# Spreading the normalisers of four heads from DRAM by two transfers, one for each query part, in place of four

## The chip, the cores and the metric

The kernel runs on one core of one Trainium2 chip. The metric is the device time of one execution in microseconds (us); lower is better. Each comparison runs the kernel before on the same chip beside the other kernel, so its median differs a little from job to job (294.9 to 301.2 us).

## The reference, cut to what matters

An attention with forget gates feeds a channel mix. Batch 8, 8 heads, 576 positions, 64 dimensions a head; the mix has 512 and 1024 channels. Only the division by the row sum matters here.

```python
scores = np.where(causal, -1e9, scale * q @ k.T + decay)
attn = np.exp(scores - scores.max(-1, keepdims=True))
attn = attn / (attn.sum(-1, keepdims=True) + 1e-09)   # the normaliser
x = (attn @ v)                  # heads side by side: (B, S, 512)
xk = mu_k * x + (1 - mu_k) * x_prev                   # and xr the same with mu_r
out = sigmoid(xr @ w_r) * (relu(xk @ w_k) ** 2 @ w_v)
```

## The kernel before

Heads go in pairs (32 pairs), and the normalisers in groups of two pairs, that is four heads. TensorE sums the weights into `den`; VectorE transposes the sums, takes reciprocals and transposes back, so that `R` holds one row of normalisers per head and query part. The product of weights and values has 64 rows (dimensions) for each of two heads, so one row of normalisers must be copied to 64 partitions. For the first two groups a matmul does that. For the other 14, `R` is stored to a DRAM tile `scr` and loaded back with each row repeated 64 times into `rb`. The queries are cut into part 0 (384 columns) and part 1 (192).

```python
PARTS = [(0, 384), (384, 192)]
QB = PARTS[0][1] // 32
mm_ring = Ring(3, [P, 512], F32, "mm", mmp)            # PSUM, three buffers
scr_ring = Ring(2, [4, 32, 32 * QB], F32, "scr", drp)  # DRAM
rb_ring = Ring(3, [P, 2, S], F32, "rb")
# ... cut ...
def spread_norm(g):
    scr = scr_ring()
    nc.sync.dma_start(out=scr.rearrange("g r c -> (g r) c"),
                      in_=R.rearrange("p a b -> p (a b)"))
    rb = rb_ring()
    for half, (q0, n) in enumerate(PARTS):
        for hh in range(2):
            nc.sync.dma_start(
                out=rb[hh * D:(hh + 1) * D, :, q0:q0 + n],
                in_=scr[2 * half + hh, 0:2, 0:n].unsqueeze(0).to_broadcast([D, 2, n]))
    for i in range(2):
        rbs[2 * g + i] = rb[:, i, :]
# ... cut ...
def values(Pi, half):
    nm = mm_ring()
    # ... cut: matmuls of weights and values into nm ...
    q0, n = PARTS[half]
    nc.vector.tensor_tensor(out=xs[Pi % NX][:, 1 + q0:1 + q0 + n], in0=nm[:, 0:n],
                            in1=rbs[Pi][:, q0:q0 + n], op=ALU.mult)
```

The multiply is L423 in the profile of the kernel before.

The softmax here doesn't subtract the row's maximum and nothing guards it: scores larger than these inputs give would overflow.

## Time and profile before

| | before |
|---|---|
| median time | 294.92 us (4 runs, 293.64 to 297.48) |
| profiled run | span 298.2 us, granted TensorE clock 0.977 |
| TensorE busy | 266.5 us, 89% |
| loads `rb<-scr` | 28 of 192 KB and 28 of 96 KB, 3.3 us to landing |
| wait of the multiply for them | 12.0 us in all |

The profiled run took 299.94 us, over 1.5% above the fastest run, so it counts as slow. In a row of the profile, `x<-mm,rb` means that the instruction writes tile `x` and reads `mm` and `rb`; the first pair of numbers is the busy time in us and the mean duration in ns, what follows the second bar is idle time of the engine just before, with what ended it. "SPq" is the queue that issues transfers.

### The profile page before, as it was taken

How to read it: one execution, taken by the hardware profiler on the slowest of the kernel's cores; microseconds unless marked ns; L12 is line 12 of the kernel's file. 1: busy time of each engine (PE TensorE's matmuls, PEld its weight loads, DVE VectorE, ACT ScalarE, POOL GpSimd, SP SyncE). 2: the span in 40 equal slices, each digit the busy share in tenths (PEclk: the TensorE clock that was granted, in tenths of full speed). 3: DMA queues.
4: the chain of work that ended last, by engine and by line, in shares of the span. 5: the costliest groups of instructions: out<-in, count | busy, mean ns of one | idle time of the engine just before them, and what ended most of it. 6: DMA issues, size and time to landing. Idle time of an engine off the chain costs nothing.

```text
span 298.2 us, 8098 instructions
## 1 busy us (share of the span) xinstructions
PE 266.5 (89%) x3194; PEld 159.0 (53%) x3221; DVE 226.1 (76%) x462; ACT 204.6 (69%) x360; POOL 88.0 (30%) x117
## 2 busy tenths in 40 slices
PE   1677878769899999999969999999989999999994
PEld 0344545335555655566535655566555656655551
DVE  6758989787978988789847977797968886874431
ACT  4878688457877878588865887688777875424530
POOL 7294227262333333223322424132322111000000
PEclk9999799978999999999988999999999999999999
DMA  7999996854759494939584594949471915131112
GB/s 211 237 258 202 242 230 190 206 142 146 208 150 262 126 300 121 282 112 270 151 240 135 150 274 119 278 114 290 115 223 65 250 35 185 65 115 70 68 41 106
DMA packets 82438, 52.06 MB, mean 175 GB/s; under 512 B 50336, under 2 KB 77216, under 8 KB 82400
## 3 DMA queue, kind: packets, MB, share of 16 engines
q1 hardware_dynamic: 80080, 48.75, 57.5%
q0 software_dynamic: 2096, 2.62, 5.1%
q8 instruction: 25, 0.41, 0.6%
q10 hardware_dynamic: 224, 0.18, 0.3%
q14 instruction: 13, 0.11, 0.1%
HBM read 41.96 MB, written 12.19 MB: 182 GB/s over the span
## 4 chain that ended last, share of the span: by engine, by line
PE 65%; DVE 11%; DMA 9%; ACT 9%; issue 2%; SPq 2%; DVEq 0%; ACTq 0%
PE mm L468 25%; PE mm L453 15%; PE mm L416 7%; PE sc L328 7%; DMA rb<-scr 6%; ACT a L334 5%; PE sc L233 4%; PE den L364 3%; PE mm L472 3%; ACT qkT L244 2%; DMA scr<-R 2%; SPq L386 2%; DVE x L423 2%; DVE a L340 2%; ACT rel L459 1%
## 5 line engine op out<-in xcount | busy, mean ns | idle before, releaser
L334 ACT ACTIVATE a<-sc 128x1024 bf16<-128x1024 f32 (+1 forms) x128 | 100.3, 842 | 17.0 <-PE sc L328 16.8
L453 PE MATMUL mm<-xk,wk_sb 128*128 128x288 bf16 x512 | 73.9, 289 | 1.5 <-DVE x L423 0.7
L468 PE MATMUL mm<-wv_sb,relusq 128*128 128x512 bf16 x246 | 61.4, 387 | 3.3 <-DVE x L423 2.7
L459 ACT ACTIVATE rel<-mm 128x288 bf16<-128x288 f32 x128 | 48.4, 417 | 16.4 <-PE mm L453 13.0
L453 PEld LDWEIGHTS <-wk_sb 128*128 128x128 bf16 x512 | 48.0, 99 | 21.0 <-issue 6.3
L220 POOL TENSOR_TENSOR vw<-vf,wbf 128x512 bf16<-128x512 f32 x32 | 34.5, 1077 | 72.8 <-DMA vf<-in_v_dram 30.1
L461 DVE TENSOR_TENSOR relusq<-rel 128x576 bf16<-128x576 bf16 x64 | 34.2, 544 | 28.0 <-ACT rel L459 27.9
L340 DVE TENSOR_TENSOR a<-a,bound 128x256 bf16<-128x256 bf16 (+2 forms) x96 | 44.7, 477 | 3.6 <-ACT a L334 3.3
L482 ACT ACTIVATE th<-mm 128x512 f32<-128x512 f32 x36 | 21.5, 598 | 34.7 <-PE mm L468 28.7
L328 PE MATMUL sc<-qkT 64*128 64x64 bf16 (+4 forms) x384 | 37.3, 291 | 8.2 <-ACT a L334 3.8
L468 PEld LDWEIGHTS <-relusq 128*128 128x128 bf16 x256 | 23.6, 99 | 32.2 <-issue 8.1
L244 ACT COPY qkT<-sc 128x1024 bf16<-128x1024 bf16 x29 | 29.4, 1014 | 14.8 <-PE sc L237 14.3
L423 DVE TENSOR_TENSOR x<-mm,rb 128x384 bf16<-128x384 f32 x64 | 27.1, 454 | 14.7 <-DMA rb<-scr 12.0
L209 POOL CAST qb<-qf 128x512 bf16<-128x512 f32 x22 | 18.1, 825 | 62.6 <-PE sc L233 37.4
L468 PE MATMUL mm<-wr_sb,xr 128*128 128x512 bf16 x111 | 32.6, 387 | 1.6 <-issue 0.3
L489 DVE SCALAR_TENSOR_TENSOR res<-th,mm 128x512 f32<-128x512 f32 x36 | 24.6, 683 | 12.4 <-PE mm L468 8.1
L328 PEld LDWEIGHTS <-qkT 64*128 64x128 bf16 x384 | 15.0, 96 | 30.3 <-issue 24.1
L416 PE MATMUL mm<-a,vw 128*32 128x192 bf16 (+3 forms) x896 | 29.5, 267 | 0.7 <-ACT rel L459 0.4
L441 DVE SCALAR_TENSOR_TENSOR xk<-diff,mu_k_sb,x 128x576 bf16<-128x576 bf16 x32 | 26.4, 826 | 1.1
L441 DVE SCALAR_TENSOR_TENSOR xr<-diff,mu_r_sb,x 128x576 bf16<-128x576 bf16 x32 | 26.0, 812 | 0.0
L416 PEld LDWEIGHTS <-vw 128*32 128x32 bf16 x896 | 20.4, 99 | 6.8 <-issue 4.4
L233 PE MATMUL sc<-ident,qb 128*128 128x128 bf16 x128 | 13.2, 230 | 8.4 <-DVE qb L209 5.3
(67 smaller groups left out, 237.0 us busy)
## 6 DMA issues: line engine op xcount, KB each, us to landing
out_dram<-res SPq DMA_DIRECT2D x36, 256.0 KB, 3.5
qf<-in_q_dram SPq DMA_DIRECT2D x32, 256.0 KB, 4.3
kf<-in_k_dram SPq DMA_DIRECT2D x32, 256.0 KB, 4.5
vf<-in_v_dram SPq DMA_DIRECT2D x64, 128.0 KB, 4.2
rb<-scr SPq DMA_DIRECT2D x28, 192.0 KB, 3.3
scr<-R SPq DMA_DIRECT2D x14, 192.0 KB, 1.9
rb<-scr SPq DMA_DIRECT2D x28, 96.0 KB, 3.3
vt_f<-in_v_dram SPq DMA_DIRECT2D x8, 128.0 KB, 5.4
```

Source lines behind the costliest of these rows:

```text
L220: nc.gpsimd.tensor_tensor(out=vw[Pi % NV], in0=vf[Pi % NV], in1=wbf[:, :4, 2 * Pi:2 * Pi + 2].unsqueeze(3).to_broadcast([P, 4, 2, D]), op= ...
L244: copy(qkT[Pi % NQK][:, lo * S:hi * S].rearrange("p (i s) -> p i s", i=n)[:, :, 0:4 * P] .rearrange("p i (j c) -> p i j c", c=4), tp[:, 4 ...
L328: nc.tensor.matmul(sc[:, hh, w:w + n], lhsT=t[lo:lo + D, S + kb * P:S + (kb + 1) * P], rhs=t[lo:lo + D, q0:q0 + n], start=True, stop=True)
L334: nc.scalar.activation(out=a[:, :, off:off + w], in_=sc[:, :, 0:w], func=AF.Exp, scale=SCALE)
L340: nc.vector.tensor_tensor(out=v_, in0=v_, in1=bound[:, o:o + w].unsqueeze(1).unsqueeze(1).to_broadcast([P, 2, n, w]), op=ALU.min)
L416: nc.tensor.matmul(nm[r0:r0 + 32, o:o + n], lhsT=w[:, d0:d0 + 32], rhs=a[:, hh, col:col + n], start=(kb == 0), stop=last, tile_position=(0 ...
L423: nc.vector.tensor_tensor(out=xs[Pi % NX][:, 1 + q0:1 + q0 + n], in0=nm[:, 0:n], in1=rbs[Pi][:, q0:q0 + n], op=ALU.mult)
L441: nc.vector.scalar_tensor_tensor(out=dst[:, p, :], in0=diff, scalar=mu[:, p:p + 1], in1=x[:, 0:S], op0=ALU.mult, op1=ALU.add)
L453: nc.tensor.matmul(kp[:, :HB], lhsT=wk_sb[:, db, fb * P:(fb + 1) * P], rhs=xks[b][:, db, hf * HB:(hf + 1) * HB], start=(db == 0), stop=(db ...
L459: nc.scalar.activation(rel[:, fb % 2, :], kp[:, :HB], func=AF.Relu)
L461: nc.vector.tensor_mul(rsq[b][:, fb - 1:fb + 1, hf * HB:(hf + 1) * HB], rel, rel)
L468: nc.tensor.matmul(ps, lhsT=tiles[b][:, i, t0:t0 + P], rhs=w[:, i, :], start=(i == 0), stop=(i == n - 1))
```

## The change

The intent is two issues in place of four for each group. A query part is fetched for both heads by one transfer onto all 128 partitions. For that, part 1 is padded to the width of part 0, so that the rows of both pairs of heads lie end to end (2 x 384 numbers, 3072 B) in DRAM and in `rb`.

```diff
-    rb_ring = Ring(3, [P, 2, S], F32, "rb")
+    rb_ring = Ring(3, [P, 2, 2, 32 * QB], F32, "rb")
 ...
-        for half, (q0, n) in enumerate(PARTS):
-            for hh in range(2):
-                nc.sync.dma_start(
-                    out=rb[hh * D:(hh + 1) * D, :, q0:q0 + n],
-                    in_=scr[2 * half + hh, 0:2, 0:n].unsqueeze(0).to_broadcast([D, 2, n]))
+        for half in range(2):
+            nc.sync.dma_start(
+                out=rb[:, half].rearrange("p j c -> p (j c)"),
+                in_=scr[2 * half:2 * half + 2, 0:2, :].rearrange("g j c -> g (j c)")
+                .unsqueeze(1).to_broadcast([2, D, 2 * 32 * QB]))
         for i in range(2):
-            rbs[2 * g + i] = rb[:, i, :]
+            rbs[2 * g + i] = rb[:, :, i, :]
 ...
-                                in1=rbs[Pi][:, q0:q0 + n], op=ALU.mult)
+                                in1=rbs[Pi][:, half, 0:n], op=ALU.mult)
```

The first four pairs and the views used at the start are adapted to the new shape in the same way (cut).

More of the change, by code (lines that the diff above doesn't have):

```diff
@@ L140 @@
     chain = [rb_ring() for _ in range(2)]
-    lf, cum, wrow, zrow = (chain[i // 2][:BH, i % 2, :] for i in range(4))
+    lf, cum, wrow, zrow = (
+        chain[i // 2].rearrange("p a b c -> p (a b c)")[:BH, i % 2 * S:i % 2 * S + S]
+        for i in range(4))
     nc.scalar.dma_start(out=lf, in_=f_bh[:, :])
@@ L397, in spread_now @@
             for i in range(2):
-                rbs[2 * g + i] = rb[:, i, :]
+                rbs[2 * g + i] = rb[:, :, i, :]
         for half, (q0, n) in enumerate(PARTS):
@@ L402, in spread_now @@
                              rhs=R.rearrange("p a b -> p (a b)")[:, 0:n], start=True, stop=True)
-            copy(rbs[Pi][:, q0:q0 + n], rp[:, 0:n])
+            copy(rbs[Pi][:, half, 0:n], rp[:, 0:n])
     def values(Pi, half):
```

## The prediction

In the text below k is the number of DMA engines that a transfer runs on. That the new form has k = 2 was supposition: nothing in the kernel before shows it. So are the reasons for the queueing and one of the three terms of the range, the one for the rate, because no trace shows them. 12.6 us of delay, less 1.5 for the work ahead, plus 1 for the queueing (a bare estimate) are 12.1 us a group; 14 groups make 169 us, and 295 + 169 = 464 was put at 460. The 28 us that it names as the new period are 15.9 + 12. The range of some -45 to +55 us came from all three terms, so it doesn't follow from the two that are left.

> **What bounds the kernel now.** I read the page of the kernel before first: engine shares, then the group of instructions that reads the tile `rb`, then the list of DMA issues.
>
> ```profile
> PE 266.5 (89%) x3194; PEld 159.0 (53%) x3221; DVE 226.1 (76%) x462; ACT 204.6 (69%) x360; POOL 88.0 (30%) x117
> ...
> L423 DVE TENSOR_TENSOR x<-mm,rb 128x384 bf16<-128x384 f32 x64 | 27.1, 454 | 14.7 <-DMA rb<-scr 12.0
> ...
> rb<-scr SPq DMA_DIRECT2D x28, 192.0 KB, 3.3
> scr<-R SPq DMA_DIRECT2D x14, 192.0 KB, 1.9
> rb<-scr SPq DMA_DIRECT2D x28, 96.0 KB, 3.3
> ```
>
> TensorE is the bound at 89%. The spread is 14 groups (four heads each) of one store `scr<-R` and four loads `rb<-scr`; one load lands 3.3 us after its issue. The multiply that eats the normalisers (L423, VectorE) already waits 12.0 us for these loads in all, so they have no slack. What such a wait does to TensorE I read from busy times by stretch, two undisturbed steady ones against one with the longest wait in it:
>
> ```profile
> core 0: us, PE busy (x) PEld busy (x) DVE busy (x) ACT busy (x) POOL busy (x), PEclk, DMA share, GB/s
> ...
> 149.31:165.90 16.59, 14.30 (x188) 7.92 (x186) 10.69 (x22) 10.62 (x20) 4.00 (x4) 0.90 0.62 176
> 182.00:215.00 33.00, 32.44 (x398) 19.28 (x401) 26.76 (x55) 25.40 (x46) 10.14 (x13) 1.00 0.70 197
> 215.00:248.00 33.00, 32.12 (x445) 19.26 (x449) 25.65 (x56) 26.02 (x48) 7.32 (x8) 1.00 0.51 145
> ```
>
> TensorE is 97 to 98% busy in the undisturbed stretches: there is no idle time in which a new delay could hide. The chain of work that ended last, at one group, shows the path:
>
> ```profile
> 144.90 0.58 DVE R L377
> ...
> 145.50 1.86 DMA scr<-R
> ...
> 147.38 0.58 SPq L386
> ...
> 149.31 5.35 DMA rb<-scr
> ...
> 154.74 0.38 DVE x L423
> ...
> 155.16 0.58 PE mm L468
> ```
>
> R is ready at 145.5, the store lands 1.86 us later, the first of four loads is issued at 147.38 and the fourth at 149.31, and it lands 5.35 us after that; the multiply frees a PSUM buffer of the ring of three and TensorE goes on. The timeline of VectorE and of the DMA queue gives the same for all groups. With t0 the start of the first load's issue, the multiply of query part 1 starts at t0 + 5.2 to 7.4 us, typically 5.7 (100.43 to 106.02, 115.43 to 121.25, 181.35 to 187.44), in 8 of 14 groups after a wait; the others have about 1 us to spare. From one t0 to the next it is (258.40 - 51.40) / 13 = 15.9 us.
>
> [...]here an issue takes 0.60 us (start-to-start 0.65) and the landing 3.3[...].
>
> **The change part by part.**
> 1. *Issues.* Two in place of four: the last one starts 2 x 0.65 = 1.3 us sooner.
> 2. *Bytes.* Query part 1 is padded from 192 to 384 columns. A group moves 2 x 384 = 768 KB in place of 2 x 192 + 2 x 96 = 576 KB; 14 groups make 2.75 MB more than now, 5% of the 52.06 MB. Rows are 3072 B in place of 1536 and 768 B: 256 in place of 512 per group.
> 3. *Engines.* This decides it. The old source pattern is [64 copies, 2, n], and the destination has 64 partitions: k = 16. The new source is [2, 64 copies, 768], and its slowest dimension is the 2 for the two heads; the destination's is 128. [...]both transfers use the same two engines, one after the other.
> 4. *Arithmetic and buffers.* The multiply, its shape, the copies of the first four pairs and the order of instructions stay. `rb` grows by 1.5 KB per partition and buffer: no time.
>
> The rate of one engine, as an estimate: I take the fastest slices of the DMA line. In 102 to 107 us (mostly loads) they are 367 to 385 GB/s, in the tail (stores only) up to 415.
>
> ```profile
> GB/s 233 295 258 246 221 270 258 320 270 197 197 135 184 141 49 86 154 123 117 98 137 111 96 156 170 178 221 279 309 352 385 352 334 324 365 367 340 324 315 291
> ...
> GB/s 306 0 0 5 11 22 5 0 38 410 251 22 0 0 0 0 0 0 0 0 0 377 322 0 0 0 0 27 377 295 0 0 0 0 38 415 246 0 0 0
> ```
>
> That is 24 to 26 GB/s per engine. A transfer of 393,216 B on two engines is 196,608 B each: 196,608 / 25,000 per us = 7.9 us. The fixed part: a 192 KB load lands in 3.0 us at the least, of which 196,608 / 385,000 = 0.5 us is data, so 2.5 us. First transfer: t0 + 2.5 + 7.9 = t0 + 10.4. Second, behind it: t0 + 18.3, against use at t0 + 5.7 now. **Delay: 12.6 us per group.**
>
> What of it reaches the end? Nearly all. VectorE works in order and stands still at L423, with masks, squares and results behind it; TensorE has the ring of three PSUM buffers, two of them held by the waiting products, so it does about one more unit. I take off 1.5 us for that work ahead. Then I add 1 us for queueing[...]. Sum: 12.6 - 1.5 + 1 = 12.1 us, times 14 groups = 169 us. 295 + 169 = 464 us; I say 460.
>
> **The rivals.**
> - *The transfers still use 16 engines* (the pattern reaches the hardware in a form with 64 or 128 outermost).[...] Then the second transfer is issued 1.3 us sooner, and of the 12.0 us of waits some 9 us go (each of the 8 waits at part 1 falls by at most 1.3, the first waits by some 0.6). Half reaches TensorE: 290 to 292 us, within 2%. I give this 13%.
> - *Padding costs.* 16 engines, but 33% more bytes in the spread land later in heavy load: 192 KB more at 375 GB/s is 0.5 us per group, at most 14 x 0.5 = 7 us, less the gain of the issues. Within 2% again.
> - *The two engines become the bound by themselves.* If all other traffic waits behind them and casts and value weights come late, the period is more than 28 us; 32 us would make 295 + 14 x 16 = 519. Against it: q, k and v are loaded two to four slots ahead of use, a slot being 8 us.
> - *The wait is hidden.* Against it: L423 already waits in most groups, and TensorE has no spare time.
>
> **Range and chances.** 460 us if k is 2. Within that case [...]the work ahead by 1.5, the queueing by -1 to +3; over 14 groups that is some -45 to +55. The range 405 to 515 leaves out the case of 16 engines, which I keep in the chances: faster 0.02, same 0.12, slower 0.86.
>
> **What would show it.** The list of issues should have `rb<-scr` x28 with 384 KB. Right: a median landing of 10 to 18 us; DMA slices of low busy share (2 of 16 engines, a tenth or two) and 50 GB/s while L423 waits; L423 waiting for `rb<-scr` some 150 to 190 us in all (12.0 now); PE busy time near 266 us, but its share falling to about 57%; t0 to t0 at 28 us. Wrong: a landing of 3 to 4 us means 16 engines, and the time stays near 291. A landing near 10 us for both would mean that they run side by side (the second on other engines), about 8 us less per group and some 350 us in all. A landing as expected, but a time well below 400, would mean that TensorE had more work ahead than I allow.

## More of the kernel before

All engines have a fixed order of work; a string of letters per step of two heads sets it. `A` is the products with the values and their multiplies, `P` the spread, `K` key units, `L` loads, `R` gate and value units.

```python
ROUND = (
    "S0 V T L R M K2 D c A G N V S1 M K2 P G H M W",
    "S0 L V K1 W M M T k K3 S1 M D V A H R",
    "S0 W G T c L M K3 G G S1 M A D N K1 G R P M H",
    "S0 V M T G W L K2 c D S1 M A R M H K2",
)
```

## The result and the profile after

| | before | after |
|---|---|---|
| median time | 294.92 us | 487.16 us (4 runs, 484.73 to 489.85) |
| granted TensorE clock, profiled run | 0.977 | 0.797 |
| TensorE busy | 266.5 us, 89% | 316.2 us, 65% |
| wait of the multiply for `rb<-scr` | 12.0 us | 183.6 us |

The change takes 1.650 times as long (95% interval 1.636 to 1.665). A ratio here is the mean time of one kernel's fast runs over that of the other's of the same rounds, so it isn't quite the ratio of the two medians.

From the page of the changed kernel: the engine shares, the granted clock in 40 slices (tenths of full speed), the multiply, and the issues of the spread.

```profile
PE 316.2 (65%) x3221; PEld 177.3 (36%) x3221; DVE 229.9 (47%) x462; ACT 207.4 (43%) x360; POOL 87.9 (18%) x117
...
PEclk9989966758597785977769577796867968688799
...
L427 DVE TENSOR_TENSOR x<-mm,rb 128x384 bf16<-128x384 f32 x64 | 28.2, 458 | 189.9 <-DMA rb<-scr 183.6
...
rb<-scr SPq DMA_DIRECT2D x28, 384.0 KB
```

The work of VectorE and ScalarE is nearly what it was (busy 226.1 and 204.6 us before, 229.9 and 207.4 after). The multiply now waits 183.6 us for the loads, and TensorE's busy time has grown by 50 us although its work is the same: by the clock records, which show full or half clock and nothing between, it ran at half clock for about 198 of the 488 us (2 x (1 - 0.797) x 487.8). The page gives no landing times any more. The chain of work that ended last gives one; this is a group at 257 us.

```profile
257.29 1.86 DMA scr<-R
...
259.16 0.54 SPq L389
...
259.76 17.54 DMA rb<-scr
...
277.39 0.37 DVE x L427
```

The second load takes 17.54 us from its issue to its landing. What moves in that time is in the DMA view of 259.16 to 277.4 us, cut into 40 slices of 0.46 us: the busy share of the 16 engines in tenths, and the rate.

```profile
DMA  0010011111111113436972111146411111665995
GB/s 0 0 13 0 40 54 47 54 47 54 54 54 54 54 52 99 171 144 229 371 240 72 54 54 54 53 138 169 129 40 54 54 54 47 180 172 216 409 402 200
```

Long runs of slices stand at a share of one tenth and at 47 to 54 GB/s, which is seven or eight packets of 3072 B in a slice. Two engines of 16 are 12.5%, and the share is 0.12 in 260.3 to 264.5 us and 0.13 in 262.0 to 266.0 us. The packet records are finer: two such packets start every 118 ns (median), which is 52 GB/s, or 26 GB/s for each of two engines. Of the 229 us in which any 3072 B packet is under way, it is two at once for 212. The trace does not number the engines. The queue's own timeline shows a second effect that the prediction did not name.

```profile
259.16 1.11 SPq L389 DMA_DIRECT2D rb<-scr  x2
260.37 4.95 SPq L120 DMA_DIRECT2D qf<-in_q_dram  x1
265.41 0.42 SPq L120 DMA_DIRECT2D kf<-in_k_dram  x1
265.93 8.14 SPq L131 DMA_DIRECT2D vf<-in_v_dram  x2
```

The issue of one query load takes 4.95 us and that of two value loads 8.14 us, where a lone one takes 0.4 to 0.6 us. In all 14 groups the longest issue among the five behind the spread takes 4.8 to 6.1 us (0.5 to 2.0 before). So while the spread moves two packets at a time, the queue takes longer to issue later transfers, and in the slices at 47 to 54 GB/s nothing else moves. GpSimd's waits for the value loads grew from 30.1 to 135.2 us in all; no run isolates what that cost.

The timelines of VectorE and of the queue give the course of every group. With t0 the start of the group's first load issue, the means over 14 groups (13 for the two last rows; differences of the unrounded means) are:

| us, profiled run | before | after | difference |
|---|---|---|---|
| t0 to the multiply of part 0 | 4.7 | 10.3 | 5.5 |
| t0 to the multiply of part 1 | 5.9 | 18.2 | 12.3 |
| from there to the next t0 | 10.0 | 11.1 | 1.1 |
| t0 to next t0 | 15.9 | 29.4 | 13.5 |

Thirteen periods of 13.5 us more make 175 us; the start is 1.4 us later and the stretch after the last t0 13.1 us longer (39.8 to 52.9). The sum, 189.7 us, is the whole difference of the spans, 487.8 - 298.2 = 189.6. So the place of the loss is known, and the experiments have to show its cause.

### The profile page after: what moved, and what is told of

It is laid out like the page before. It is cut to its first block, busy times and chain, and to the rows that moved or that the text cites. A ratio compares the mean times of both kernels' runs of the same rounds, so it can differ in the third digit from the quotient of the medians.

```text
span 487.8 us, 8095 instructions
## 1 busy us (share of the span) xinstructions
PE 316.2 (65%) x3221; PEld 177.3 (36%) x3221; DVE 229.9 (47%) x462; ACT 207.4 (43%) x360; POOL 87.9 (18%) x117
## 2 busy tenths in 40 slices
DMA packets 78014, 54.81 MB, mean 112 GB/s; under 512 B 49496, under 2 KB 69208, under 8 KB 77976
## 4 chain that ended last, share of the span: by engine, by line
DMA 57%; PE 22%; DVE 12%; ACT 5%; issue 2%; SPq 1%; DVEq 0%; ACTq 0%
DMA rb<-scr 50%; PE mm L472 8%; DMA scr<-R 6%; PE mm L457 5%; PE mm L420 3%; DVE x L427 2%; PE sc L331 2%; ACT a L337 2%; DVE R L380 2%; DVE xr L445 2%; DVE dT L378 2%; PE sc L236 1%; ACT qkT L247 1%; SPq L389 1%; PE den L367 1%
## 5 line engine op out<-in xcount | busy, mean ns | idle before, releaser
L457 PE MATMUL mm<-xk,wk_sb 128*128 128x288 bf16 x512 | 88.6, 325 | 68.6 <-DVE x L427 64.1
L427 DVE TENSOR_TENSOR x<-mm,rb 128x384 bf16<-128x384 f32 x64 | 28.2, 458 | 189.9 <-DMA rb<-scr 183.6
L472 PE MATMUL mm<-wv_sb,relusq 128*128 128x512 bf16 x256 | 77.1, 456 | 51.2 <-DVE x L427 51.2
L457 PEld LDWEIGHTS <-wk_sb 128*128 128x128 bf16 x512 | 53.3, 108 | 97.1 <-issue 77.8
L223 POOL TENSOR_TENSOR vw<-vf,wbf 128x512 bf16<-128x512 f32 x32 | 35.3, 1102 | 175.4 <-DMA vf<-in_v_dram 135.2
L247 ACT COPY qkT<-sc 128x1024 bf16<-128x1024 bf16 x29 | 29.4, 1013 | 73.4 <-PE sc L240 72.9
L472 PEld LDWEIGHTS <-relusq 128*128 128x128 bf16 x256 | 27.2, 111 | 90.9 <-issue 73.7
L472 PE MATMUL mm<-wr_sb,xr 128*128 128x512 bf16 x128 | 37.4, 419 | 20.1 <-DVE x L427 20.1
L331 PE MATMUL sc<-qkT 64*128 64x64 bf16 (+4 forms) x384 | 40.8, 318 | 6.5 <-ACT a L337 4.2
L420 PE MATMUL mm<-a,vw 128*32 128x192 bf16 (+3 forms) x896 | 33.5, 293 | 4.0 <-DVE x L427 4.0
L212 POOL CAST qb<-qf 128x512 bf16<-128x512 f32 x22 | 15.6, 707 | 85.2 <-PE sc L236 33.0
L445 DVE SCALAR_TENSOR_TENSOR xr<-diff,mu_r_sb,x 128x576 bf16<-128x576 bf16 x32 | 29.1, 909 | 0.0
L331 PEld LDWEIGHTS <-qkT 64*128 64x128 bf16 x384 | 15.8, 102 | 32.0 <-issue 26.8
L420 PEld LDWEIGHTS <-vw 128*32 128x32 bf16 x896 | 22.5, 108 | 12.1 <-issue 9.9
L367 PE MATMUL den<-a,E 128*2 128x192 bf16 (+4 forms) x512 | 20.6, 279 | 7.1 <-DVE a L343 7.1
```

Source lines behind the costliest of these rows:

```text
L223: nc.gpsimd.tensor_tensor(out=vw[Pi % NV], in0=vf[Pi % NV], in1=wbf[:, :4, 2 * Pi:2 * Pi + 2].unsqueeze(3).to_broadcast([P, 4, 2, D]), op= ...
L247: copy(qkT[Pi % NQK][:, lo * S:hi * S].rearrange("p (i s) -> p i s", i=n)[:, :, 0:4 * P] .rearrange("p i (j c) -> p i j c", c=4), tp[:, 4 ...
L331: nc.tensor.matmul(sc[:, hh, w:w + n], lhsT=t[lo:lo + D, S + kb * P:S + (kb + 1) * P], rhs=t[lo:lo + D, q0:q0 + n], start=True, stop=True)
L420: nc.tensor.matmul(nm[r0:r0 + 32, o:o + n], lhsT=w[:, d0:d0 + 32], rhs=a[:, hh, col:col + n], start=(kb == 0), stop=last, tile_position=(0 ...
L445: nc.vector.scalar_tensor_tensor(out=dst[:, p, :], in0=diff, scalar=mu[:, p:p + 1], in1=x[:, 0:S], op0=ALU.mult, op1=ALU.add)
L457: nc.tensor.matmul(kp[:, :HB], lhsT=wk_sb[:, db, fb * P:(fb + 1) * P], rhs=xks[b][:, db, hf * HB:(hf + 1) * HB], start=(db == 0), stop=(db ...
```

## The experiments

**Theory.** The source pattern of the changed transfer, [2 heads, 64 copies, 768], has 2 as its slowest dimension, and that is why it runs on two DMA engines: a supposition, which the runs have to test. **Rivals.** It is the padded bytes or the long rows; or two transfers in place of four, with too little in flight; or the copying dimension in the middle.

### e1: two transfers, one for each head

```diff
-        for half in range(2):
+        for hh in range(2):
             nc.sync.dma_start(
-                out=rb[:, half].rearrange("p j c -> p (j c)"),
-                in_=scr[2 * half:2 * half + 2, 0:2, :].rearrange("g j c -> g (j c)")
-                .unsqueeze(1).to_broadcast([2, D, 2 * 32 * QB]))
+                out=rb[hh * D:(hh + 1) * D].rearrange("p a j c -> p a (j c)"),
+                in_=scr.rearrange("(a g) r c -> g a r c", g=2)[hh, :, 0:2, :]
+                .rearrange("a j c -> a (j c)").unsqueeze(0)
+                .to_broadcast([D, 2, 2 * 32 * QB]))
```

Same number of transfers, bytes and rows as the change; the slowest dimension is 64 in place of 2. One thing more differs: each load carries both query parts of one head, so part 0 has to wait for both loads.

> Two transfers again, with the same 2 x 384 KB and the same 3072 B rows as the change, but one for each head of a pair: source [64 copies, 2 query parts, 768] onto 64 partitions. Theory (the engine count follows the slowest dimension; 64 gives 16 engines): the loads land in about 4 us, the multiply of query part 1 starts some 4.5 to 5.5 us after the first issue, the time is 290 to 298 us. Rival (two large padded transfers are slow in themselves, by their number, bytes or row length): stays near 487 us, above 400 in any case.

Measured: 330.82 us against 301.19, ratio 1.098 (1.090 to 1.106). The rival is out: most of the loss is gone with the same number, bytes and rows. But the theory's figure is missed as well.

```profile
rb<-scr SPq DMA_DIRECT2D x28, 384.0 KB, 5.3
```

A load lands 5.3 us after its issue where about 4 was expected, and the multiplies of parts 0 and 1 start 7.0 and 7.4 us after t0.

### e2 to e4 and e8: the same four transfers with 64, 8, 4 and 2 as the slowest dimension

In e2 each transfer is one head and one part, padded, [64 copies, 768]:

```diff
+            for hh in range(2):
+                nc.sync.dma_start(
+                    out=rb[hh * D:(hh + 1) * D, half].rearrange("p j c -> p (j c)"),
+                    in_=scr[2 * half + hh, 0:2, :].rearrange("j c -> (j c)")
+                    .unsqueeze(0).to_broadcast([D, 2 * 32 * QB]))
```

In the others only the way in which the 64 copies are counted changes; addresses, bytes, rows and results are the same. For 4:

```diff
-                    .unsqueeze(0).to_broadcast([D, 2 * 32 * QB]))
+                    .unsqueeze(0).unsqueeze(0).to_broadcast([4, D // 4, 2 * 32 * QB]))
```

> Four transfers of [64 copies, 768] in place of two, with the padded bytes and 3072 B rows of the change. Theory: 16 engines, the last load is issued 1.95 us after the first and lands some 3.8 us later, 294 to 302 us (0 to 2% over before, for the 33% more bytes). Rival (padding and long rows cost the time): near 487 us. Rival (fewer transfers in flight cost it): also near 295, so this run and e1 have to be read together.

> As e2, but the 64 copies are written as 4 x 16, so that only the shape of the source changes: slowest dimension 4. Theory: 4 engines at about 27 GB/s, 786,432 B / 4 / 27,000 = 7.3 us, last landing at 2.5 + 7.3 = 9.8 us after the first issue plus some 0.5 of other traffic, against use at 5.7 in the kernel before: 4.6 us x 14 = 64 us, so 350 to 370 us. Rival (the shape of the pattern doesn't matter, only bytes, rows or number): same as e2.

> As e3 with 2 x 32 copies: slowest dimension 2. Theory: two engines, the same 14.6 us of data as the change though there are four transfers, so within 2% of the change: 478 to 497 us, and a mean granted clock near 0.8. Rival (it is the number of transfers, or the second dimension's step of 0 behind a stepped first one): same as e2, near 297 us.

> As e2 with 8 x 8 copies: slowest dimension 8. Theory: 8 engines with 32 packets of 3072 B each per group, at some 165 ns (between the 153 measured on 4 and the 180 on 16 engines) 5.3 us, landing at 2.5 + 5.3 = 7.8 us after the first issue, 2.1 us after the use in the kernel before; 14 x 2.1 = 30 us, so 1.06 to 1.12 of before. Rival (shape does not matter): 1.02, as e2.

| run | copies counted as | ratio to before (95%) | median us | t0 to multiply of part 1, us | clock |
|---|---|---|---|---|---|
| e2 | 64 | 1.021 (1.013 to 1.028) | 307.48 | 6.5 | 0.983 |
| e8 | 8 x 8 | 1.174 (1.164 to 1.184) | 349.44 | 9.1 | 0.941 |
| e3 | 4 x 16 | 1.314 (1.304 to 1.323) | 395.46 | 12.0 | 0.887 |
| e4 | 2 x 32 | 1.668 (1.657 to 1.679) | 500.94 | 19.1 | 0.788 |

A way of writing the same copies moves the time from 307 to 501 us. Padding and row length are thereby worth 2% (e2), and the number of transfers is not the cause (e4 has four and is slower than the change). Nor is a copying dimension in the middle: e8 has one too and takes 349 us. All four missed their ranges upwards: e2 by 5 us and e4 by 4 us (on their chip the kernel before was slower too, 301.19 against 294.92, and as ratios both are about where they should be), e3 by 25 us and e8 with 1.174 against 1.06 to 1.12. The transfers on 4 and 8 engines landed later than I had worked out, from 27 GB/s an engine for e3 (half of the 54 GB/s of the slices above) and from 165 ns a packet for e8. The packet records of the trace say why: a 3072 B packet takes 130 ns in the mean in the change, 134 in e4, 153 in e3, 188 in e8 and 180 in e2. So from 2 to 8 engines each packet took longer, and on 16 about what it took on 8. For e3 that gives 64 x 0.153 = 9.8 us on each engine and 2.5 fixed, 12.3 against 12.0 measured; for e8 32 x 0.188 + 2.5 = 8.5 against 9.1.

How many engines took part can be estimated from the page, from the line with the number of packets. These are the lines of e2, e8, e3, e4 and of the change in this order.

```profile
DMA packets 78854, 54.82 MB, mean 179 GB/s; under 512 B 50336, under 2 KB 70048, under 8 KB 78816
```

```profile
DMA packets 78406, 54.82 MB, mean 158 GB/s; under 512 B 49888, under 2 KB 69600, under 8 KB 78368
```

```profile
DMA packets 78182, 54.81 MB, mean 139 GB/s; under 512 B 49664, under 2 KB 69376, under 8 KB 78144
```

```profile
DMA packets 78070, 54.81 MB, mean 110 GB/s; under 512 B 49552, under 2 KB 69264, under 8 KB 78032
```

```profile
DMA packets 78014, 54.81 MB, mean 112 GB/s; under 512 B 49496, under 2 KB 69208, under 8 KB 77976
```

The data packets are the same, yet 448, 672 and 784 are missing, all of them packets of 4 B in the packet records. In the packet records of the change each of the two loads of the last group, beside which little else moves, ends with two 4 B packets, as many as data packets were under way at once. The kernel before has 840 more packets under 512 B than the change (50,336 against 49,496), which is 56 x 16 - 28 x 2: 16 for each of its 56 spread transfers, where up to 16 of their 1536 B packets and at times a few more are under way at once. I therefore count one 4 B packet for each engine that takes part; that is my reading of these records, no view says it. There are 56 spread transfers in e2, e8, e3 and e4, and the counts come out exactly: 56 x (16 - 8) = 448, 56 x (16 - 4) = 672, 56 x (16 - 2) = 784. By this count the transfers ran on 16, 8, 4 and 2 engines. The change has 78,014, and 28 transfers on two engines make 56 such packets where e4's 56 make 112: 78,070 - 56 = 78,014. The 4 B packets of e1 (448 fewer than in e2: half as many transfers, all on 16) and of e9 below (420 fewer: 14 transfers on 2 engines and 28 on 16) fit too. With the two packets at once and the rate of 52 GB/s, that shows that the change ran on two engines.

### e9: half of the change

Part 0 by one transfer of the change, part 1 by two transfers as before.

```diff
+        nc.sync.dma_start(
+            out=rb[:, 0].rearrange("p j c -> p (j c)"),
+            in_=scr[0:2, 0:2, :].rearrange("g j c -> g (j c)")
+            .unsqueeze(1).to_broadcast([2, D, 2 * 32 * QB]))
+        n = PARTS[1][1]
+        for hh in range(2):
+            nc.sync.dma_start(
+                out=rb[hh * D:(hh + 1) * D, 1, :, 0:n],
+                in_=scr[2 + hh, 0:2, 0:n].unsqueeze(0).to_broadcast([D, 2, n]))
```

> Half of the change alone: query part 0 by the one transfer of the change (slowest dimension 2), query part 1 by two transfers of [64 copies, 2 pairs, 192] as before. Theory: 64 packets on each of two engines at 130 ns are 8.3 us, landing at 10.8; part 1 has 16 engines [...]and lands at about 11.2 in place of use at 5.7: 5.5 x 14 = 77 us, 1.22 to 1.32 of before. Rival (a fixed cost of the form, whatever the number of such transfers): 1.6.

Measured: 404.17 us against 299.2, ratio 1.357 (1.345 to 1.369), above the range. The step of the loads was right: part 1 is used 11.6 us after t0 (11.2 expected), and its two loads, which have 64 as their slowest dimension, land 10.5 us after their issue, where the same form took 3.3 us before; here the load on two engines is issued ahead of them. What came on top is the stretch from there to the next t0, 11.7 us in place of 10.0. The same shows in e1 (10.8, against 10.0 in e2): where both parts become free at once, no unit of TensorE runs between them, and the rest takes longer. That reading is argued from these runs; none was made for it alone, and the lower clock (0.873 in e9, 0.951 in e1, 0.983 in e2) is a rival that stays open. The rival of a fixed cost of the form (1.6) is out.

### e5 and e6: the clock

e5 is the change again, as the partner of e6. e6 puts useless matmuls into the waits of TensorE; their results are overwritten or never read, and the outputs are right. The 3.4 us that the expectation gives for 60 of them are an estimate from the kernel before: at full clock its groups of four 128x128 matmuls start 0.22 to 0.23 us apart (36.08, 36.30 and 36.53 us).

```diff
+    def idle_work(t):
+        for _ in range(60):
+            nc.tensor.matmul(t, lhsT=ident, rhs=ident, start=True, stop=True)
 # in values(), after the matmuls of part 1 of a group's first pair, into free columns:
+            idle_work(nm[:, 256:384])
 # and in the second buffer of the ring taken after that, ahead of its own matmuls
```

> The change itself once more, as the partner of e6 on the same chip: 1.64 to 1.66 times the kernel before, mean clock about 0.80.

> The change, with 60 useless matmuls of 128x128 put into each of the two waits of TensorE per group (28 x 60 matmuls, some 3.4 us each time at full clock), so that the granted clock stays up; the loads are untouched. Theory A (part of what the prediction lacked, 487 against 460, is the lower clock, 0.80, after the waits): mean clock above 0.92, the stretch from the multiply of part 1 to the next first issue falls from 11.2 to about 10 us, and the time to 0.950 to 0.982 of e5. Rival B (that stretch is set by VectorE, 8.8 of its 10 us busy, and by transfers queued behind the spread): clock up, but the time at 0.985 to 1.01 of e5.

Measured on one chip: e5 485.87 us, ratio 1.631 (1.621 to 1.640), clock 0.797; e6 477.23 us, ratio 1.602 (1.593 to 1.612), clock 0.935. e6 is 0.983 of e5, a hair outside what theory A expects (0.982) and below rival B's 0.985; the intervals of the two ratios do not touch. In e5 the stretch from the multiply of part 1 to the next t0 is 11.0 us and in e6 10.4; 13 x 0.54 = 7 of the 8.6 us gained lie there. t0 to the multiply of part 1 is 18.0 us in both. So keeping the clock up gave back some 8.6 us of some 190. The low clock may have cost more: e6 raised it only to 0.935, and the useless matmuls take time themselves where they outlast a wait. No run measures that.

Busy times by stretch of the change, two pieces of one group's wait and two stretches after a multiply, show the clock as the loads are waited for and after:

```profile
core 0: us, PE busy (x) PEld busy (x) DVE busy (x) ACT busy (x) POOL busy (x), PEclk, DMA share, GB/s
265.00:268.00 3.00, 0.28 (x6) 0.10 (x1) 0.00 (x0) 2.20 (x3) 0.00 (x0) 1.00 0.39 137
270.50:276.00 5.50, 4.29 (x17) 2.03 (x16) 0.00 (x0) 1.14 (x2) 0.00 (x0) 0.50 0.35 107
248.70:259.16 10.46, 10.41 (x115) 5.64 (x116) 8.75 (x18) 5.50 (x11) 2.42 (x2) 0.85 0.45 129
277.75:287.82 10.07, 9.42 (x84) 5.09 (x84) 8.78 (x17) 4.02 (x8) 2.57 (x3) 0.59 0.46 130
```

In the two pieces of the wait VectorE is at 0.00: it stood still at the multiply, as the prediction said. TensorE is busy for 4.29 us at half clock between the two loads. What half clock does shows in the same eight matmuls, in that wait and one period later at full clock:

```profile
270.26 3.57 PE L472 MATMUL mm<-wv_sb,relusq 128*128 128x512 bf16 x8 [4.98 <-DVE x L427]
287.07 1.90 PE L472 MATMUL mm<-wv_sb,relusq 128*128 128x512 bf16 x8
```

The stretches between the multiply and the next t0 have clocks of 0.85 and 0.59, and VectorE is busy 8.8 us in each: about what it has there in the kernel before (8.86 of 10.75 us in 121.60 to 132.35). So all of that work comes after the wait, as it did before.

### e7: each copy reads another row

e1 had left open why loads on 16 engines land late. Here the source of e1 is replaced by 64 different rows of `scr` (the edit against e1).

```diff
-                in_=scr.rearrange("(a g) r c -> g a r c", g=2)[hh, :, 0:2, :]
-                .rearrange("a j c -> a (j c)").unsqueeze(0)
+                in_=scr.rearrange("g r c -> (g r c)").rearrange("(d x) -> d x", d=D)
+                .unsqueeze(1)
                 .to_broadcast([D, 2, 2 * 32 * QB]))
```

> As e1 (two transfers, one for each head, 16 engines; 1.098 of before, loads landing after 5.3 us where 4 were expected, its 3072 B packets taking 195 ns in the mean against 130 in the change), but each of the 64 copies reads another 3072 B of the scratch tile in place of all the same 6 KB; the outputs are wrong on purpose. Theory (16 engines that read the same few KB of DRAM at once slow each other): packets of 3072 B fall to 121 to 140 ns, the landing to 4 to 4.5 us, the time to 1.00 to 1.05 of before. Rival (waiting for both loads before part 0, and 33% more bytes, are all of e1's loss): landing stays above 5 us and the time at 1.08 to 1.11 of before.

Measured: 316.67 us against 298.91, ratio 1.064 (1.056 to 1.073); landing 4.7 us; the 3072 B packets took 197 ns in the mean, no less than e1's 195. It lies between the two, and the packet times, which were to decide, did not fall. So fetching the same few KB again is at most a part of it (1.098 against 1.064). Why packets from `scr` take longer when 16 engines fetch them stays open.

### e10: a form without padding, two loads by head

The scratch holds 576 columns for each head and pair; two stores of 64 rows fill it and two loads of [64 copies, 1152] bring it back.

```diff
+        rows = scr.rearrange("h r c -> (h r) c")           # scr: [2, 32, S]
+        for half, (q0, n) in enumerate(PARTS):
+            nc.sync.dma_start(out=rows[:, q0:q0 + n],
+                              in_=R.rearrange("p a b -> p (a b)")[64 * half:64 * half + 64, 0:n])
+        for hh in range(2):
+            nc.sync.dma_start(
+                out=rb[hh * D:(hh + 1) * D].rearrange("p j c -> p (j c)"),
+                in_=scr[hh, 0:2, :].rearrange("j c -> (j c)").unsqueeze(0)
+                .to_broadcast([D, 2 * S]))
```

> Candidate to beat both: the scratch keeps 576 columns for a head and pair (two stores of 64 rows), and two loads of [64 copies, 1152] bring it back, one for each head: 16 engines, no padding, two issues fewer, one store more. Theory: a load lands 0.65 us for the second issue + 2.5 + some 2.2 us of data (4608 B packets, slowed as in e1) = 5.3 us after the first issue, 0.4 us sooner than part 1 of before, but part 0 now waits for both, and the second store takes 0.4: 0.99 to 1.05 of before. Rival (sharing the landing costs as much as in e1): 1.05 to 1.10.

Measured: 308.21 us against 299.2, ratio 1.034 (1.027 to 1.040): within the expectation, and slower than the kernel before.

### e11 and e12: the values later in a step

Most of the waits that the kernel before has fall into the last of the four steps of a round. Both runs are the kernel before with `A` moved in that step only.

```diff
-        "S0 V M T G W L K2 c D S1 M A R M H K2",
+        "S0 V M T G W L K2 c D S1 M R A M H K2",   # e11
+        "S0 V M T G W L K2 c D S1 M K2 A R M H",   # e12
```

> The kernel before with its four transfers, and in the last of the four steps of a round the products with the values moved behind the gate and value units (about 2 us later), so that the loads have landed when the multiply comes: most of the 8 groups that wait are of this step. If the 12.0 us of waits reach TensorE, they fall to 3 to 6 us and the time to 0.975 to 0.99 of before; if TensorE works ahead through waits this short (at 185 us it shows no idle time beside waits of 0.57 and 1.39 us), 0.99 to 1.01.

> As e11, with two key units put ahead of the products instead, which changes what follows less. The same two expectations: 0.975 to 0.99, or 0.99 to 1.01.

Measured against 297.05 us: e11 295.71 us, ratio 0.998 (0.993 to 1.003), waits 7.5 us; e12 295.67 us, ratio 1.000 (0.994 to 1.005), waits 5.6 us. The waits went down from 12.0 and the time stayed. Other waits of VectorE grew by about as much (in e12, 27.9 to 32.9 us for ScalarE's `rel` and 8.1 to 10.9 for TensorE's `mm` of L468). So these waits of up to 2.8 us did not hold the kernel up, which suggests that the fewer issues could have brought nearly nothing. It is not a rule for all short waits: in e2 they went up to 21.0 us, and the time by 2%. No version here beats the kernel before.

## Why the prediction was right, point by point

1. **Two engines: right.** Two packets of 3072 B are under way at once for 212 of 229 us, and the count of 4 B packets fits. In e4, e3, e8 and e2, with the destination left alone, that count went with the slowest dimension of the source (2, 4, 8 and 64): 784, 672 and 448 fewer than with 64. The two loads run one after the other, as predicted: the multiplies that use them start at t0 + 10.3 and 18.2 us.
2. **The delay of the loads: right, with two terms off that cancel, which is luck.** Part 1 was expected at t0 + 18.3 us and came at 18.2. By the packet records a group's 256 packets run from t0 + 1.3 to 17.6 us in the mean, 16.3 us, where 15.8 was predicted: 26 GB/s an engine at the median pace and 24 with the pauses. Other traffic does not show in that rate: the two engines together moved 48.0 GB/s of the spread while no other packet was under way and 49.5 while four to eight were. The fixed part was 1.3 us before them and 0.6 from the last to the multiply, 1.9 in place of 2.5. The 1 us of queueing that the sum had on its own is not seen: the issue waits 23.5 us in all for the stores, 22.7 before.
3. **The work ahead: wrong.** The step "I take off 1.5 us for that work ahead", with 1 us of queueing added, made -0.5 us for the stretch after the multiply. It is +1.1 us (10.0 to 11.1). A group so cost 13.5 us in place of 12.1; 14 x 1.4 us is 20 of the 27 us between 460 and 487, another 4 are the rounding from 464 to 460. TensorE does run a unit in the wait, but VectorE's 8.8 us of work in the stretch all remain. Of the +1.1 us the clock accounts for some 0.5 (e6); the rest is open, and the late transfers are one candidate.
4. **The clock: not foreseen.** I expected TensorE's busy time to stay near 266 us and its share to fall to 57%; they were 316 us and 65%. The clock fell to 0.80. The trace of the change has 28 gaps of TensorE of 3.0 to 7.4 us in the 14 groups and 21 stretches at half clock of 3.4 to 17.1 us; a gap of 4.98 us is followed by 0.50 in the stretch 270.50 to 276.00. How long a gap has to be is not shown by these traces: in e1, five of the ten gaps of 2.0 to 3.0 us in the groups came with half clock, in the gap or just after it; in the kernel before a gap of 1.9 us at 153.2 us did (3.4 us of it from 154.95), while its stretches of 3.4 us at 32.1 us and 6.8 us at 62.8 us came without any gap over 1.5 us. e6 got some 8.6 us back.
5. **The wait of the multiply:** 150 to 190 us expected, 183.6 measured.
6. **The rivals:** 16 engines did not come about. Padding alone costs 2% (e2), near the 7 us given for it. The two engines as a bound in themselves, at a period of 32 us, did not come about either: it was 29.4, above the 28 expected. A wait that is hidden is out, by the 183.6 us.

## What to carry to other kernels

Before two transfers are made one, look at the outermost dimension of the pattern. Here a 2 in the source's (two heads) went with two packets under way at a time and 52 GB/s, even though the transfer writes all 128 partitions; with four transfers of the same bytes and 2, 4, 8 and 64 there, the kernel took 501, 395, 349 and 307 us. (Only the source's was varied in these runs.) Order the pattern so that the dimension with many elements comes first, or leave the split. And a short wait may be free (e11), whereas a later landing in each group cost its full length and more: in e8, e3 and the change part 1 was used 3.2, 6.1 and 12.3 us later, and the period grew by 3.7, 7.0 and 13.5 us.
